# Lightning attention and a feed-forward network: the states of the first groups in PSUM banks of their own, decayed from PSUM, with a new order of operations

## The chip, the cores and the metric

The kernel runs on one core of one Trainium2 chip. The metric is device time in microseconds (us), lower is better. A core has five engines with an instruction queue each: TensorE (PE in the profile, and PEld for its weight loads), VectorE (DVE), ScalarE (ACT), GpSimd (POOL) and SyncE (SP, which here issues most transfers). They share the on-chip memory SBUF. TensorE writes its products to PSUM, which holds eight banks here; VectorE and ScalarE can read PSUM.

A time of a run is some 1.7 to 2 us longer than its span, which goes from the first to the last instruction. Each run records the mean granted clock of TensorE, 1.0 being full speed.

## The reference

Attention without softmax, in blocks, with a decayed state; then a feed-forward network with the activation h + sin²(alpha·h)/alpha. Cut to what matters:

```python
# q, k, v: 4 batches x 8 heads x 768 positions x 64;  lam: one decay per head
for b in range(nb):                                   # blocks of 64 positions
    intra = einsum(einsum(qb, kb) * Dmask, vb)        # inside the block
    inter = einsum(qb * lam_pow, kv_state)            # what earlier blocks left
    out[:, :, block] = intra + inter
    kv_state = lam**64 * kv_state + einsum(kb * rev_pow, vb)

x = out, as 3072 rows x 512
h = x @ w_in                                          # 512 -> 2048
g = h + sin(alpha * h)**2 / alpha
return g @ w_out                                      # 2048 -> 512
```

## The kernel before

The kernel works in 24 attention units of 4 heads by 256 positions (two chunks of 128, numbered 0 and 1). Four units make a group of 512 rows, and each of the six groups goes through the feed-forward network. Nothing is scheduled automatically: one list, ORDER, gives every operation, its engine and its place, and each engine takes its own operations in that order. A wait of one operation therefore holds up everything behind it on that engine.

An entry is `operation.indices:engine:bank`, with engines V (VectorE), G (GpSimd), A (ScalarE), T (TensorE), S (SyncE). The names that the text uses are these:

| entry | what it does |
|---|---|
| `ld`, `wi`, `wo` | loads of q, k, v of a unit; of a quarter of w_in; of a quarter of w_out |
| `sq`, `sk`, `cv` | scale q and k by powers of lam, cast v to bf16 |
| `tq`, `tk`, `tcq`, `tck` | turn q and k on TensorE, and copy the result out of PSUM (`tdq`, `tdk`: turn by DMA) |
| `s`, `m` | scores (16 matmuls), and their mask on VectorE |
| `k`, `kc` | matmuls of the chunks' states, and their copy from PSUM to SBUF |
| `a.u.c`, `n.u.c` | add the earlier state and decay it for the output; make the state that the next chunk takes |
| `o`, `x` | output of the unit, and its copy to the rows that the network reads |
| `f1`, `sin`, `sqr`, `stt`, `f2` | first product, sine, square, the rest of the activation, second product (`f1a`: half of an `f1`, with the first two units of a group alone) |
| `w.n` | n filler matmuls on zeros, whose result nobody reads |

Before, the states of both chunks are written into a spare part of `okv`, a pair of PSUM banks (one for each chunk) that the outputs use too. They are copied to SBUF together, and everything after that has SBUF inputs:

```python
def kvmm(u, **_):
    okv[u] = ps.tile([P, 2, 512], FP32, name="okv", tag="okv", bufs=1)
    ...                                                # 16 matmuls into okv[u]

def kv_copy(u, eng, **_):
    kva[u] = kvp.tile([P, 2, 2, D], FP32, name=f"kva{b}{hh}", bufs=1)
    copy(eng, kva[u][:, :n]..., okv[u][:, :n, 2 * P:3 * P])      # both chunks

def kv_decayed(u, c, eng, **_):
    x = kva[u][:, c]                                   # in SBUF
    if prev is not None:
        eng.tensor_tensor(out=t[:], in0=x, in1=prev[:], op=ALU.add)
        x = t[:]
    eng.tensor_tensor(out=kvbd[u, c][:], in0=x..., in1=LBD..., op=ALU.mult)

def load(u, j, **_):
    loads[u, j] = nc.sync.dma_start(...)
    if 4 <= u < 8 and j == 0 and mlp[0] is not None:   # mlp: the last feed-forward
        after(loads[u, j], mlp[0])                     # matmul written so far
```

In ORDER the units of group 1 (4 to 7) are mixed into group 0 and into the first product, and several state operations and scalings stand on VectorE while GpSimd works too. The loads of units 4 to 7 come early and don't wait, since no feed-forward matmul stands before them. The quarters of w_in are spread out:

```
... m.1.1:V wi.0:G w.3:T:okv o.0:T ... k.3:T a.1.0:V sk.4:V sq.4:G ... wi.1:G tck.3:V
s.3:T k.4:T tcq.4:V kc.4:A ... n.1.0:V a.4.0:G ... o.3:T s.4:T x.3.0:V x.3.1:A
f1a.0.0:T:1 f1.0.0:T f1a.0.1:T:3 sq.6:G m.4.0:V m.4.1:V wi.2:G sk.6:G tq.5:T:0 ...
```

Of the kernel before, what the change touches and what calls it, by code (L numbers as in the profile page):

```python
# [11 lines left out]
FP32 = mybir.dt.float32  # L12
# [6 lines left out]
ld.0.0:S ld.0.1:S ld.0.2:S ld.1.0:S ld.1.1:S ld.1.2:S ld.2.0:S ld.2.1:S ld.2.2:S ld.3.0:S sq.0:G  # L19
ld.3.1:S ld.3.2:S ld.4.0:S ld.4.1:S tq.0:T:2 sk.0:V tk.0:T:0 sq.1:V cv.0:A sk.1:G tables:V k.0:T  # L20
cv.1:G sq.2:G tq.1:T:3 kc.0:V tcq.1:V sk.2:G w.5:T:h1 tk.1:T:1 tck.1:A k.1:T tcq.0:V tck.0:V s.0:T
m.0.0:V a.0.0:G m.0.1:V kc.1:V tq.2:T:0 w.4:T:h2 tk.2:T:2 cv.2:A k.2:T kc.2:A tck.2:A s.1:T ld.4.2:S
ld.5.0:S ld.5.1:S sq.3:V ld.5.2:S ld.6.0:S ld.6.1:S cv.3:G ld.6.2:S ld.7.0:S ld.7.1:S ld.7.2:S
ld.8.0:S sk.3:G tcq.2:A m.1.0:V m.1.1:V wi.0:G w.3:T:okv o.0:T x.0.0:V tq.3:T:3 tcq.3:A w.3:T:s0
s.2:T w.4:T:okv k.3:T a.1.0:V sk.4:V sq.4:G tk.3:T:3 m.2.0:V m.2.1:V kc.3:A w.3:T:okv o.1:T cv.4:A
x.1.0:A tq.4:T:0 a.3.0:G a.2.0:G sk.5:G wi.1:G tck.3:V s.3:T k.4:T tcq.4:V kc.4:A n.0.0:G tk.4:T:2
m.3.0:V tck.4:A sq.5:G m.3.1:V w.3:T:okv o.2:T a.0.1:G n.1.0:V a.4.0:G cv.5:G x.2.0:A w.5:T:okv
o.3:T s.4:T x.3.0:V x.3.1:A f1a.0.0:T:1 f1.0.0:T f1a.0.1:T:3 sq.6:G m.4.0:V m.4.1:V wi.2:G sk.6:G
tq.5:T:0 f1a.0.2:T:2 tk.5:T:5 f1.0.1:T cv.6:G tcq.5:V f1.0.2:T sin.0.0:A n.2.0:G sqr.0.0:A a.1.1:V
sq.7:G stt.0.0:V sin.0.1:A sqr.0.1:V sin.0.2:A sqr.0.2:A n.1.1:G n.4.0:G k.5:T stt.0.1:V tck.5:V  # L30
kc.5:V stt.0.2:V f1a.0.3:T:4 f1.0.3:T f1.0.4:T:0 sin.0.3:A sin.0.4:A sqr.0.3:A sqr.0.4:V wi.3:G
f1.0.5:T:1 stt.0.3:V sin.0.5:A sk.7:G wo.0:G f1.0.6:T:3 stt.0.4:V a.5.0:G sqr.0.5:A f1.0.7:T:2 s.5:T
k.6:T stt.0.5:V sin.0.6:A sqr.0.6:A kc.6:V m.5.0:V tq.6:T:0 tcq.6:A sin.0.7:A sqr.0.7:A w.4:T:okv
o.4:T stt.0.6:V m.5.1:V stt.0.7:V x.4.0:A cv.7:A tk.6:T:4 f1.0.8:T:1 f1.0.9:T:0 k.7:T tq.7:T:3
kc.7:V ld.8.1:S ld.8.2:S tcq.7:V tk.7:T:2 ld.9.0:S tck.6:A sin.0.8:A sqr.0.8:V s.6:T sin.0.9:A
m.6.0:V tck.7:A o.5:T m.6.1:V wo.1:G n.3.0:G a.7.0:G sqr.0.9:A ld.9.1:S ld.9.2:S ld.10.0:S ld.10.1:S
x.5.0:A stt.0.8:V f1.0.10:T:3 stt.0.9:V f1.0.11:T:2 a.6.0:G s.7:T sin.0.10:A o.6:T sin.0.11:A
m.7.0:V sqr.0.10:A f1.0.12:T:1 f1.0.13:T:0 sqr.0.11:G sq.8:G sin.0.12:A x.6.0:A sin.0.13:A
f1.0.14:T:4 sin.0.14:A stt.0.10:V m.7.1:V sqr.0.12:V sqr.0.13:G stt.0.11:V stt.0.12:V stt.0.13:V
o.7:T sqr.0.14:G f1.0.15:T:3 stt.0.14:V x.7.0:A f1a.1.0:T:5 f1.1.0:T sin.0.15:A sqr.0.15:A sin.1.0:A  # L40
f1a.1.1:T:2 f1.1.1:T f1a.1.2:T:1 f1a.1.3:T:4 f1.1.2:T sqr.1.0:A sin.1.1:A sin.1.2:A sqr.1.1:A
n.7.0:V stt.0.15:V a.3.1:V sqr.1.2:A n.5.0:G sk.8:G n.0.1:G f2.0.1.0:T:0 stt.1.0:V f1.1.3:T wo.2:G
f1.1.4:T:3 sin.1.3:A f1.1.5:T:5 stt.1.1:V sqr.1.3:A sin.1.4:A sqr.1.4:A stt.1.2:V stt.1.3:V
f2.0.2.0:T:2 a.4.1:G sq.9:G cv.8:G stt.1.4:V k.8:T wo.3:G n.6.0:G sk.9:G tdq.8:S sin.1.5:A
f2.0.1.1:T tdq.9:S tdk.8:S cv.9:A sqr.1.5:A stt.1.5:V f1.1.6:T:4 sin.1.6:A f1.1.7:T:3 sin.1.7:A
f2.0.0.0:T:1 f2.0.0.1:T f1.1.8:T:5 sqr.1.6:A sq.10:G sk.10:G stt.1.6:V kc.8:V a.8.0:G sin.1.8:A
sqr.1.7:A ld.10.2:S cv.10:G a.2.1:V sqr.1.8:A stt.1.7:V a.5.1:V a.7.1:V stt.1.8:V f2.0.1.2:T k.9:T
kc.9:A f2.0.0.2:T f2.0.0.3:T ld.11.0:S n.8.0:G n.4.1:G tdk.9:S ld.11.1:S ld.11.2:S oc.0.0:A
ld.12.0:S ld.12.1:S f1.1.9:T:3 f2.0.1.3:T sin.1.9:A k.10:T s.8:T n.3.1:V sqr.1.9:A tdq.10:S
f1.1.10:T:1 f2.0.2.1:T stt.1.9:V m.8.0:V n.2.1:V tdk.10:S ld.12.2:S sk.11:G sq.11:G tdq.11:S  # L50
tdk.11:S f2.0.2.2:T ld.13.0:S m.8.1:V cv.11:A kc.10:A sin.1.10:A ld.13.1:S ld.13.2:S ld.14.0:S
oc.0.1:V f1.1.11:T:3 k.11:T sin.1.11:A sqr.1.10:A sqr.1.11:A sk.12:G kc.11:A s.9:T m.9.0:V m.9.1:V
f2.0.2.3:T stt.1.10:V f2.0.3.0:T:0 cv.12:A oc.0.2:A st.0.2.0:S ld.14.1:S s.10:T ld.14.2:S st.0.1.0:S
a.10.0:G sq.12:G a.9.0:G o.8:T m.10.0:V x.8.0:V m.10.1:V f2.0.3.1:T f1.1.12:T:1 stt.1.11:V o.9:T
sin.1.12:A x.9.0:V n.5.1:G s.11:T a.11.0:G ld.15.0:S ld.15.1:S ld.15.2:S f1.1.13:T:2 o.10:T sk.13:G
sin.1.13:A x.10.0:A m.11.0:V m.11.1:V cv.13:A sqr.1.12:A f1.1.14:T:3 a.8.1:G f1.1.15:T:5 sin.1.14:A
sqr.1.13:A sin.1.15:A sq.13:G a.6.1:V ld.16.0:S ld.16.1:S tdq.12:S ld.16.2:S o.11:T f2.0.3.2:T
sq.14:G sk.14:G x.11.0:V f2.0.3.3:T stt.1.12:V stt.1.13:V oc.0.3:V sqr.1.14:A k.12:T kc.12:A
f1.2.0:T:4 f1.2.1:T:2 stt.1.14:V f1.2.2:T:1 sqr.1.15:G stt.1.15:V f1.2.3:T:3 f1.2.4:T:0 n.9.0:G
sin.2.0:A sin.2.1:A sqr.2.0:A stt.2.0:V sin.2.2:A sqr.2.1:A stt.2.1:V cv.14:G sk.15:G sin.2.3:A  # L60
k.13:T ld.17.0:S tdk.12:S kc.13:V sk.16:G sin.2.4:A sqr.2.2:A stt.2.2:V sqr.2.3:G n.11.0:G ld.17.1:S
stt.2.3:V f1.2.5:T:4 sqr.2.4:A stt.2.4:V n.6.1:V n.10.0:G f1.2.6:T:5 sin.2.5:A f1.2.7:T:2 f1.2.8:T:1
f1.2.9:T:3 sq.15:G a.12.0:G n.12.0:G f2.1.0.0:T:0 f2.1.0.1:T sq.16:G sin.2.6:A sin.2.7:A sqr.2.5:A
sin.2.8:A sqr.2.6:A sqr.2.7:A stt.2.5:V stt.2.6:V sin.2.9:A sqr.2.8:A sqr.2.9:G n.7.1:G st.0.0.0:S
a.13.0:G cv.15:G tdq.13:S stt.2.7:V k.14:T s.12:T ld.17.2:S tdk.13:S m.12.0:V m.12.1:V f2.1.0.2:T
tdq.14:S tdq.15:S st.0.0.1:S kc.14:A f2.1.0.3:T o.12:T sq.17:G ld.18.0:S a.10.1:G stt.2.8:V
stt.2.9:V s.13:T a.12.1:G f2.1.1.0:T:2 a.14.0:G n.8.1:G x.12.0:V st.0.2.1:S tdk.14:S m.13.0:V
f1.2.10:T:1 f1.2.11:T:3 tdq.16:S st.0.1.1:S m.13.1:V oc.1.0:V tdk.15:S tdk.16:S st.0.3.0:S o.13:T
ld.18.1:S ld.18.2:S ld.19.0:S ld.19.1:S ld.19.2:S ld.20.0:S ld.20.1:S s.14:T x.13.0:A cv.16:A
m.14.0:V f2.1.1.1:T sin.2.10:A m.14.1:V f2.1.1.2:T k.15:T kc.15:V sqr.2.10:G stt.2.10:V sq.18:G  # L70
f1.2.12:T:0 sin.2.11:A sqr.2.11:A stt.2.11:V n.12.1:G tdq.17:S f2.1.1.3:T cv.17:A oc.1.1:A o.14:T
s.15:T m.15.0:V n.14.0:G f1.2.13:T:3 sin.2.12:A sqr.2.12:A a.15.0:G a.9.1:G tdq.18:S x.14.0:V
f1.2.14:T:2 ld.20.2:S ld.21.0:S ld.21.1:S ld.21.2:S k.16:T f1.2.15:T:1 stt.2.12:V m.15.1:V
f2.1.2.0:T:0 kc.16:A o.15:T f2.1.2.1:T f2.1.2.2:T f2.1.2.3:T sin.2.13:A sqr.2.13:A sin.2.14:A
a.16.0:G x.15.0:A sqr.2.14:G stt.2.13:V n.10.1:G sk.17:G stt.2.14:V f1.3.0:T:2 k.17:T n.13.0:G
cv.18:G sq.19:G n.15.0:G s.16:T st.1.1.0:S sin.2.15:A sqr.2.15:A stt.2.15:V oc.1.2:V f1.3.1:T:0
sin.3.0:A sin.3.1:A sqr.3.0:A sqr.3.1:A a.15.1:G f2.1.3.0:T:3 f2.1.3.1:T tdk.17:S st.0.3.1:S sk.18:G
tdq.19:S f2.1.3.2:T n.9.1:G m.16.0:V a.14.1:G f2.1.3.3:T m.16.1:V f1.3.2:T:1 kc.17:A k.18:T
stt.3.0:V stt.3.1:V s.17:T m.17.0:V m.17.1:V sin.3.2:A a.11.1:G sk.19:G sqr.3.2:G cv.19:G f1.3.3:T:0
f1.3.4:T:2 f1.3.5:T:4 oc.1.3:A sin.3.3:A sqr.3.3:A kc.18:V n.11.1:G n.15.1:G stt.3.2:V stt.3.3:V  # L80
f1.3.6:T:3 f1.3.7:T:1 f1.3.8:T:5 sin.3.4:A sqr.3.4:A sin.3.5:A sqr.3.5:G stt.3.4:V sin.3.6:A
sqr.3.6:G stt.3.5:V stt.3.6:V sin.3.7:A st.1.2.0:S st.1.0.0:S o.16:T ld.22.0:S ld.22.1:S f1.3.9:T:0
f1.3.10:T:4 f2.2.0.0:T:2 f2.2.0.1:T f1.3.11:T:3 f2.2.0.2:T sqr.3.7:A ld.22.2:S st.1.0.1:S ld.23.0:S
ld.23.1:S ld.23.2:S cv.20:A stt.3.7:V x.16.0:V sin.3.8:A sqr.3.8:A sin.3.9:A stt.3.8:V sqr.3.9:A
stt.3.9:V a.18.0:G f2.2.0.3:T k.19:T sin.3.10:A a.13.1:G a.17.0:G sin.3.11:A sqr.3.10:G tdk.19:S
stt.3.10:V sqr.3.11:A st.1.3.0:S tdk.18:S kc.19:V s.18:T m.18.0:V stt.3.11:V sq.20:G f2.2.1.0:T:0
o.17:T sk.20:G sk.21:G x.17.0:A m.18.1:V f1.3.12:T:1 f1.3.13:T:3 f2.2.1.1:T st.1.3.1:S s.19:T
m.19.0:V sq.21:G o.18:T f2.2.1.2:T sq.22:G sk.22:G f1.3.14:T:4 x.18.0:V k.20:T kc.20:V cv.21:A
sin.3.12:A oc.2.0:A f1.3.15:T:2 k.21:T sqr.3.12:G sin.3.13:A sin.3.14:A n.13.1:G sqr.3.13:G
f2.2.1.3:T a.19.0:G m.19.1:V kc.21:A sqr.3.14:A stt.3.12:V a.20.0:G stt.3.13:V tdq.20:S n.14.1:G  # L90
# [33 lines left out]
def kernel(  # L124
# [11 lines left out]
    nc = tc.nc  # L136
# [464 lines left out]
```

## Time and profile before

| | before |
|---|---|
| timed runs | 231.43 us, median of 3 (230.57 to 232.22) |
| profiled run | 228.56 us, span 226.8 us, clock 0.992 |
| TensorE busy | 211.3 us, 93% of the span |
| first feed-forward matmul | 25.59 us |

From the profile page of the kernel before: busy time of each engine; below it the span in 40 slices of 5.67 us, a digit being the busy share in tenths, and for PEclk the granted clock in tenths.

```profile
PE 211.3 (93%) x2081; PEld 110.3 (49%) x2111; DVE 139.2 (61%) x231; ACT 126.3 (56%) x219; POOL 135.5 (60%) x195
...
PE   8587877999999999989999999999999999999993
...
DVE  3979699788578977867546755256583563524020
...
PEclk9969999999999999999999999999999999999999
```

TensorE is the limit, and it is full nearly everywhere but in the first seven slices (to 40 us). In the third slice the clock was cut: the 6 is a stretch of half clock.

The timeline of VectorE in the kernel before, from 16 to 32 us: start, duration in us, engine, line, operation, output<-inputs, their shapes and the number of instructions; in brackets the idle time before it and what ended it.

```profile
17.08 1.86 DVE L398 TENSOR_TENSOR kvbd<-kva,LBD 128x256 bf16<-128x256 f32 x1
...
22.79 1.20 DVE L406 TENSOR_TENSOR kvs<-kva,LHP 128x128 f32<-128x128 f32 x1
...
27.85 3.12 DVE L394 TENSOR_TENSOR kvx<-kva,kvs 128x128 f32<-128x128 f32 x1
31.01 0.42 DVE L398 TENSOR_TENSOR kvbd<-kvx,LBD 128x256 bf16<-128x256 f32 x1
```

The timeline of GpSimd in the same kernel from 26 to 32 us, with the same columns:

```profile
27.87 1.05 POOL L277 TENSOR_TENSOR KD<-st_k,R 128x512 bf16<-128x512 f32 x1
28.86 0.62 POOL L270 CAST VB<-st_v 128x512 bf16<-128x512 f32 x1
29.43 0.40 POOL L406 TENSOR_TENSOR kvs<-kva,LHP 128x128 f32<-128x128 f32 x1
29.79 1.03 POOL L277 TENSOR_TENSOR QL<-st_q,E 128x512 bf16<-128x512 f32 x1
```

The same decay took 1.86 us once and 0.42 us the other time. The addition at 27.85 us took 3.12 us, about as long as four GpSimd instructions that followed each other without a gap (27.87 to 30.82 us). The Trainium skill, page "SBUF — State Buffer", section "Who interferes with whom", says that a VectorE instruction with two inputs in SBUF contends with a GpSimd instruction that reads SBUF, and that one with at most one SBUF input, outside the two-port modes, doesn't. The trace agrees.

The timeline of TensorE in the kernel before, from 24 to 34 us:

```profile
25.59 1.59 PE L453 MATMUL hps<-xt,w_in_sb 128*128 128x256 bf16 x12
...
30.64 1.04 PE L453 MATMUL hps<-xt,w_in_sb 128*128 128x512 bf16 x3 [0.47 <-DMA w_in_sb<-in_moe_w_in_dram]
32.15 1.02 PE L453 MATMUL hps<-xt,w_in_sb 128*128 128x512 bf16 x4 [0.47 <-DVE gall L487]
```

The first product begins at 25.59 us, mixed with group 1, and waits for a piece of w_in and then for VectorE, whose late `stt` (gall) hold the PSUM banks.

### The profile page before, as it was taken

Reading aid. Unit: us, or ns where it says so; the run is one execution under the profiler, and the core shown is the slowest. Engines: PE = TensorE matmul, PEld = TensorE weight load, DVE = VectorE, ACT = ScalarE, POOL = GpSimd, SP = SyncE. Lnnn points to the kernel's source line nnn. Section 1 sums busy time; section 2 is a strip of 40 time slices with the busy share of each in tenths; the row PEclk is TensorE's granted clock in tenths of the full one; section 3 lists DMA queues with packets and bytes.
Section 4 is the critical chain, followed back from the end, with each engine's and each line's share of the span. In section 5 each row is a group of like instructions: output and inputs, shape, how many; then the busy total and the mean of one; then the engine's idle time right before and its main releaser. Section 6 shows DMA issues by size and latency. Waiting matters only on the chain.

```text
span 226.8 us, 5334 instructions
## 1 busy us (share of the span) xinstructions
PE 211.3 (93%) x2081; PEld 110.3 (49%) x2111; DVE 139.2 (61%) x231; ACT 126.3 (56%) x219; POOL 135.5 (60%) x195
## 2 busy tenths in 40 slices
PE   8587877999999999989999999999999999999993
PEld 6365644565444544544444444444555444444452
DVE  3979699788578977867546755256583563524020
ACT  2234468989667479644648853468345376553101
POOL 5669994389656799897897999246152153530000
PEclk9969999999999999999999999999999999999999
DMA  5999999956999999798999915504015022132235
GB/s 140 291 293 242 268 268 251 216 110 99 141 258 182 289 287 202 180 134 219 220 248 260 194 27 111 112 13 90 21 28 116 3 46 46 25 72 46 44 71 117
DMA packets 63849, 33.92 MB, mean 150 GB/s; under 512 B 19648, under 2 KB 60880, under 8 KB 63824
## 3 DMA queue, kind: packets, MB, share of 16 engines
q1 hardware_dynamic: 59344, 29.31, 58.5%
q0 software_dynamic: 4224, 4.19, 11.5%
q8 instruction: 16, 0.26, 0.5%
q10 hardware_dynamic: 256, 0.08, 0.2%
q14 instruction: 9, 0.07, 0.1%
HBM read 27.28 MB, written 6.29 MB: 148 GB/s over the span
## 4 chain that ended last, share of the span: by engine, by line
PE 77%; DVE 9%; DMA 4%; POOL 3%; issue 2%; ACT 2%; SPq 1%; DVEq 0%; ACTq 0%; POOLq 0%
PE ops L496 33%; PE hps L453 31%; PE okv L430 3%; PE sp L345 3%; DMA QT<-KD 2%; PE okv L421 2%; PE okv L376 2%; DVE gall L487 2%; DMA lam_bc<-in_lam_dram 2%; PE ops L519 2%; DVE kvx L394 1%; PE bz L563 1%; DVE ST L355 1%; DVE kvbd L398 1%; POOL QL L277 1%
## 5 line engine op out<-in xcount | busy, mean ns | idle before, releaser
L487 DVE SCALAR_TENSOR_TENSOR gall<-s,r_sb,hps 128x512 bf16<-128x512 bf16 x96 | 69.4, 743 | 41.7 <-POOL s L482 23.0
L453 PE MATMUL hps<-xt,w_in_sb 128*128 128x512 bf16 (+1 forms) x399 | 89.9, 362 | 2.2 <-DVE gall L487 0.9
L473 ACT ACTIVATE s<-hps,alpha_sb 128x512 bf16<-128x512 f32 x96 | 64.8, 686 | 40.7 <-PE hps L453 35.7
L496 PE MATMUL ops<-w_out_sb,gall 128*128 128x512 bf16 x355 | 84.4, 379 | 1.3 <-issue 0.9
L482 POOL TENSOR_TENSOR s<-s 128x512 bf16<-128x512 bf16 x32 | 33.1, 1041 | 45.0 <-ACT s L473 44.8
L453 PEld LDWEIGHTS <-w_in_sb 128*128 128x128 bf16 x416 | 38.7, 98 | 41.4 <-issue 1.2
L496 PEld LDWEIGHTS <-gall 128*128 128x128 bf16 x368 | 34.7, 98 | 40.6
L355 DVE TENSOR_TENSOR ST<-sp,mask 128x512 bf16<-128x512 f32 x48 | 31.5, 683 | 13.6 <-PE sp L345 13.5
L480 ACT ACTIVATE s<-s 128x512 bf16<-128x512 bf16 x60 | 36.6, 626 | 1.2 <-DVE gall L487 0.4
L277 POOL TENSOR_TENSOR KD<-st_k,R 128x512 bf16<-128x512 f32 x22 | 22.9, 1045 | 5.5 <-DMA st_k<-in_k_dram 4.2
L277 POOL TENSOR_TENSOR QL<-st_q,E 128x512 bf16<-128x512 f32 x22 | 22.9, 1044 | 0.4 <-DVE E L217 0.3
L268 ACT COPY ob<-ops 128x512 f32<-128x512 f32 (+1 forms) x14 | 7.8, 554 | 23.4 <-PE ops L496 14.0
L398 POOL TENSOR_TENSOR kvbd<-kvx,LBD 128x256 bf16<-128x256 f32 x26 | 16.1, 619 | 2.0
L268 ACT CAST xt<-okv 128x512 bf16<-128x512 f32 (+1 forms) x15 | 8.5, 568 | 13.6 <-PE okv L430 11.6
L270 DVE COPY ob<-ops 128x512 f32<-128x512 f32 x11 | 7.5, 685 | 13.2 <-PE ops L496 13.1
L394 POOL TENSOR_TENSOR kvx<-kva,kvs 128x128 f32<-128x128 f32 x26 | 12.2, 468 | 3.8 <-DVE kva L270 2.0
L345 PE MATMUL sp<-QT 64*64 64x128 bf16 x384 | 10.4, 226 | 2.3 <-DVE QT L270 1.3
L268 ACT CAST VB<-st_v 128x512 bf16<-128x512 f32 x13 | 8.0, 615 | 6.7 <-DMA st_v<-in_v_dram 6.7
L430 PE MATMUL okv<-ST,VB 64*64 64x128 bf16 x384 | 10.0, 222 | 0.0
L345 PEld LDWEIGHTS <-QT 64*64 64x64 bf16 x384 | 6.9, 111 | 5.3 <-issue 2.5
L376 PEld LDWEIGHTS <-KD 64*64 64x64 bf16 x320 | 5.2, 109 | 8.1 <-issue 3.6
L270 POOL CAST VB<-st_v 128x512 bf16<-128x512 f32 x11 | 6.7, 612 | 3.7 <-DMA st_v<-in_v_dram 3.7
(60 smaller groups left out, 138.0 us busy)
## 6 DMA issues: line engine op xcount, KB each, us to landing
st_q<-in_q_dram SPq DMA_DIRECT2D x24, 256.0 KB, 5.5
st_k<-in_k_dram SPq DMA_DIRECT2D x24, 256.0 KB, 5.4
st_v<-in_v_dram SPq DMA_DIRECT2D x24, 256.0 KB, 5.2
out_dram<-ob SPq DMA_DIRECT2D x46, 128.0 KB, 2.4
w_in_sb<-in_moe_w_in_dram POOLq DMA_DIRECT2D x4, 512.0 KB, 8.8
w_out_sb<-in_moe_w_out_dram POOLq DMA_DIRECT2D x4, 512.0 KB, 9.3
QT<-QL SPq DMA_TRANSPOSE x16, 3.9
QT<-KD SPq DMA_TRANSPOSE x16, 3.9
```

What stands on the lines that cost most here:

```text
L268: nc.scalar.copy(out=out, in_=in_)
L277: eng.tensor_tensor(out=t[:], in0=stage[u, j][:].rearrange("p h two e -> p two h e"), in1=tab[:, :, hh * HH:(hh + 1) * HH].unsqueeze(3).to ...
L345: nc.tensor.matmul(out=sp[hd][half[c], par, hp, :], lhsT=QT[half[hd], 1, par, hp, half[c]], rhs=QT[half[hd], 0, :, hp, half[c]], start=Tru ...
L355: nc.vector.tensor_tensor(out=stm[u][:, hd], in0=sps[u][hd][:], in1=mask[:].unsqueeze(2).to_broadcast([P, 2, 2, P]), op=ALU.mult)
L398: eng.tensor_tensor(out=kvbd[u, c][:], in0=x.unsqueeze(2).to_broadcast([P, 2, 2, D]), in1=LBD[:, 2 * hh:2 * hh + 2, :].unsqueeze(3).to_bro ...
L430: nc.tensor.matmul(out=okv[u][half[hd], c, hp * P:(hp + 1) * P], lhsT=VB[half[c], par, 2 * hp + hd, :], rhs=ST[half[c], hd, par, hp, :], s ...
L453: mlp[0] = nc.tensor.matmul(out=hps[g, f][:].rearrange("p (b i) -> p b i", b=2)[:, bs] .rearrange("p b i -> p (b i)"), lhsT=w_in_sb[:, c, ...
L473: nc.scalar.activation(out=s1[g, f][:], in_=hps[g, f][:], func=ACTF.Sin, scale=alpha_sb[:, f:f + 1])
L480: nc.scalar.activation(out=s2[g, f][:], in_=x[:], func=ACTF.Square)
L482: eng.tensor_tensor(out=s2[g, f][:], in0=x[:], in1=x[:], op=ALU.mult)
L487: nc.vector.scalar_tensor_tensor(out=gall[g][:, f, :], in0=s2.pop((g, f))[:], scalar=r_sb[:, f:f + 1], in1=hps.pop((g, f))[:], op0=ALU.mul ...
L496: mlp[0] = nc.tensor.matmul(out=ops[g, m][:], lhsT=gall[g][:, f, m * P:(m + 1) * P], rhs=w_out_sb[:, f, :], start=(f == 0), stop=(f == NFC ...
```

## The change

The intent: take work from the port that VectorE and GpSimd share, and get group 0 finished sooner. The diff, cut to its core:

```diff
-    XSPLIT = (3,)
+    HOLD = (0, 1)
+    XSPLIT = (2, 3)
 ...
-    nc.scalar.dma_start(out=lam_bc[:], in_=lam.partition_broadcast(P))
+    nc.sync.dma_start(out=lam_bc[:], in_=lam.partition_broadcast(P))
 ...
+    (tables LHP, LBD, and later alpha_sb, r_sb: now made at the start,
+     before, by an operation "tables" in ORDER)
 ...
-        if 4 <= u < 8 and j == 0 and mlp[0] is not None:
-            after(loads[u, j], mlp[0])
+        if (u, j) == (4, 0):
+            after(loads[u, j], f1mm[HOLD])
 ...
-    def kvmm(u, **_):
-        okv[u] = ps.tile([P, 2, 512], FP32, name="okv", tag="okv", bufs=1)
+    def kvmm(u, bank, **_):
+        if u < 8:
+            kps[u] = [psum([P, P], FP32, "kvp", i)[:] for i in bank]
+        else:
+            okv[u] = ps.tile([P, 2, 512], FP32, name="okv", tag="okv", bufs=1)
+            kps[u] = [okv[u][:, c, 2 * P:3 * P] for c in range(2)]
 ...
     def kv_decayed(u, c, eng, **_):
-        x = kva[u][:, c]
+        if u < 8 and c == 0:
+            x = kps[u][0].rearrange("p (hp e) -> p hp e", hp=2)
+        else:
+            x = kva[u][:, c]
```

The copy `kc.u.c` of units 0 to 7 now takes one chunk, and the output copies of unit 2 are split by chunk, as those of unit 3 were. ORDER is new throughout. Units 0 to 3 are all but finished before the first product; units 4 to 7 stand inside the second product of group 0; loads of unit 4 and later wait until the fourth matmul of `f1.0.1`, so the quarters of w_in, now issued one after the other, have the DMA engines with less company. The head of the new order, cut:

```
... k.0:T:3,0 tck.0:V sk.1:V s.0:T a.0.0:V m.0.0:V ... k.1:T:2,1 s.1:T o.0:T sk.2:G kc.0.0:A sq.2:V ...
... m.2.1:V wi.0:G wi.1:G a.0.1:G wi.2:G wi.3:G k.2:T:0,1 ... f1a.0.0:T:4 o.3:T f1a.0.1:T:3 ...
f1.0.6:T:3 f1.0.7:T:0 f1.0.8:T:1 f1.0.9:T:4 f1.0.10:T:2 ... ld.4.0:S ld.4.1:S ld.4.2:S ...
... f2.0.2.0:T:2 tq.4:T:5 f2.0.0.0:T:3 ... k.4:T:3,0 ... o.4:T ... o.7:T ... f1a.1.0:T:4 ...
```

## The prediction

> **What bounds the kernel now.** TensorE. The page gives PE 211.3 us busy of a 226.8 us span (93%). The groups and the chain of waits give throughputs: four 512-column matmuls take 0.86 us, so both feed-forward products need 768 x 0.2155 = 165.5 us. An attention unit costs about 0.35 (scores) + 0.65 (output) + 0.25 (states), times 24; transposes 3.5 us: useful PE work is about 199 us. The tail after the last matmul is 3.9 us. About 23.5 us is lost, 7.4 before the first transpose.
>
> Counting matmuls by stretch of time, 29.3 us of useful work is done by 50.2 us: 13.5 us is lost between 7.4 and 50.2, some 3 us in the remaining 170. The first feed-forward matmul starts at 25.6 us.
>
> **Why the head is slow.** In the timeline VectorE is nearly dense from 6.5 to 37 us, with instructions stretched: one 128x128 state addition took 3.12 us (GpSimd's are 0.47), a state decay 1.86 (GpSimd 0.62), a key scaling 1.35 (another 0.68), a 64x4 copy 1.03 (its twin 0.16). Each overlaps GpSimd instructions. This agrees with the Trainium skill, page "SBUF — State Buffer", section "Who interferes with whom": VectorE instructions with two SBUF inputs, or in a two-port mode, and GpSimd block each other. The excess sums to about 7 us by 31 us.
>
> **What the change does.** In groups 0 and 1 VectorE decays the first state straight from PSUM (estimate 0.42 us) without waiting for the copy; state additions go to GpSimd; two banks per unit free the output's bank. The tables move before the first scaling, where VectorE waits for GpSimd's first scaling (to about 7.3 us): the first key scaling comes 1 us later. Group 0 now precedes the first product, which runs almost unmixed; group 1 is mixed into the second. Loads of units 4 to 7 wait for an early feed-forward matmul, so w_in lands sooner.
>
> VectorE's list up to group 0's last masks sums to 14 us. From 7.3 us, by hand, group 0 ends and full feed-forward starts near 22 to 23 us, with 7.3 us of useful work done: 7.5 to 8.5 us lost, against about 11 lost at 25.6 us before. Gain: 2.5 to 3.5 us. The unmixed first product (16 x 0.86 = 13.8 us) balances ScalarE at about 13.7, so about 1 us is lost. Group 1 amid the second product is VectorE-dense and lies at the edge of DMA: loads of eight units and both weights need about 51 us of all DMA engines (shares of the queue table), so unit 7 lands about 48. I expect 2 to 3 us lost there, as before from 25.6 to 50. The rest stays within 1.5 us.
>
> **Predicted: 228.5 us (225.0 to 231.8).** Faster by over 2%: 0.28; within 2%: 0.69; slower: 0.03.
>
> **What would show it.** Right: no VectorE state instruction above 0.8 us before 40 us; VectorE's busy time falls by about 7 us; full feed-forward starts at 21.5 to 23.5 us; PE stays above 97% after 60 us. Wrong: feed-forward starting at 25 us or later, PE waiting for w_in between 22 and 33 us, or for unit 6 or 7 loads between 42 and 52 us.
>
> **What would make it wrong.** The VectorE chain may be latency-bound, delaying the head; group 1 may fit perfectly under the second product (then 225 or below); the granted clock (0.66 at 10 to 15 us) may change; new stalls later.

## The result, and the profile after

| | before | after |
|---|---|---|
| timed runs, median | 231.74 us (230.57 to 232.22, 4 runs) | 223.67 us (222.35 to 224.02, 4 runs) |
| ratio, with 95% interval | | 0.9649 (0.9594 to 0.9703) |
| profiled run | 228.56 us, span 226.8, clock 0.992 | 223.69 us, span 221.9, clock 1.000 |

Ratios here and below are the mean time of one kernel's fast runs over that of the other's of the same rounds, so they are not quite the ratio of the medians quoted. The change is faster by 3.5%, some 8 us, and lies below the predicted range. The profiled runs alone show only 4.9 us of it.

From the profile page of the kernel after, the lines that answer to those above (a slice is 5.55 us):

```profile
PE 208.5 (94%) x2081; PEld 109.3 (49%) x2111; DVE 128.0 (58%) x220; ACT 129.6 (58%) x234; POOL 132.2 (60%) x200
...
PE   8689999799999999999979999999999999999992
...
DVE  3996698158699758674658475757531362580020
...
PEclk9999999999999999999999999999999999999999
```

TensorE is full from the fourth slice on, but for two slices at seven tenths: the 8th (39 to 44 us) and the 21st (111 to 117 us), which before were nearly full at these places. The clock is never cut, and VectorE is busy 11.2 us less.

The state tiles of the kernel after, `kvp` in PSUM: all decays that read them, with minimum, median and maximum in ns and the first and last start.

```profile
L420 DVE TENSOR_TENSOR kvbd<-kvp,LBD x8: 408/416/425, 10.0 to 53.6; 128x256 bf16<-128x256 f32 x8
```

All eight took 0.41 to 0.43 us, six of them (at 10.01 and 19.86 us and the four of group 1, from 47.73 us on) beside GpSimd instructions: the case with one SBUF input doesn't contend, as the page says. The run a_decay_sbuf below shows the same decays from SBUF. One blocked instruction is left on VectorE; its timeline from 9 to 13 us:

```profile
10.01 0.42 DVE L420 TENSOR_TENSOR kvbd<-kvp,LBD 128x256 bf16<-128x256 f32 x1
10.34 1.28 DVE L364 TENSOR_TENSOR ST<-sp,mask 128x512 bf16<-128x512 f32 x2
11.54 1.45 DVE L286 TENSOR_TENSOR QL<-st_q,E 128x512 bf16<-128x512 f32 x1
```

The scaling of q at 11.54 us has two SBUF inputs and runs beside a scaling on GpSimd (11.39 to 12.43 us); its twin at 8.47 us took 0.68.

TensorE of the kernel after, timeline from 18 to 46 us:

```profile
20.16 0.60 PE L475 MATMUL hps<-xt,w_in_sb 128*128 128x256 bf16 x4
...
21.15 13.79 PE L475 MATMUL hps<-xt,w_in_sb 128*128 128x256 bf16 x75
34.78 1.03 PE L518 MATMUL ops<-w_out_sb,gall 128*128 128x512 bf16 x3
...
41.31 3.61 PE L518 MATMUL ops<-w_out_sb,gall 128*128 128x512 bf16 x15 [1.25 <-DMA w_out_sb<-in_moe_w_out_dram]
```

From 21.15 us the first product runs in one piece without a wait, and the second begins where it ends. One wait of 1.25 us for the last w_out follows.

### Where TensorE loses time, stage by stage

To compare two orders, I credited each matmul in the trace with its time at full throughput (0.2155 us per 512 columns, 0.35 us per 16 score or output matmuls, 0.25 us per 16 state matmuls, fillers nothing). This sums to 195.6 us for either kernel. "Lost" is the clock on the wall less the useful work done, cut at fixed amounts of useful work. The first 8 us of useful work are about group 0 and its transposes; from 8 to 20 is the first product, mixed with group 1 in the order before; from 20 to 44 the second product. The tail after the last matmul, about 4 us in both, is left out.

```
lost us     to first    to 8     to 20    to 44    to 62    to       sum
            transpose   useful   useful   useful   useful   end
before        7.41      11.07     4.09     0.57     0.47     3.44    27.0   (profiled run)
c_before      7.46      14.34     3.76     0.57     0.47     4.24    30.8   (before, run again)
after         6.90       7.66     0.13     2.03     0.78     4.69    22.2
c_after       6.97       7.65     0.13     2.70     0.78     5.19    23.4   (after, run again)
```

Against the profiled run of before, the head gained 3.9 us with its start, the first product 4.0, and 3.0 were given back later. Against a more usual run of before (the next section), the head gained 7.2.

### The profile page after: what moved, and what is told of

It is laid out like the page before. It is cut to its first block, busy times and chain, and to the rows that moved or that the text cites. A ratio compares the mean times of both kernels' runs of the same rounds, so it can differ in the third digit from the quotient of the medians.

```text
span 221.9 us, 5359 instructions
## 1 busy us (share of the span) xinstructions
PE 208.5 (94%) x2081; PEld 109.3 (49%) x2111; DVE 128.0 (58%) x220; ACT 129.6 (58%) x234; POOL 132.2 (60%) x200
## 4 chain that ended last, share of the span: by engine, by line
PE 74%; DMA 12%; POOL 4%; issue 3%; SPq 2%; DVE 1%; ACT 1%; POOLq 0%; ACTq 0%
PE ops L518 31%; PE hps L475 29%; DMA w_out_sb<-in_moe_w_out_dram 6%; PE okv L452 3%; PE sp L354 3%; DMA QT<-QL 2%; PE okv L443 2%; PE bz L576 2%; PE ops L541 2%; PE pt L313 2%; DMA st_k<-in_k_dram 2%; SPq L533 1%; PE okv L390 1%; DMA lam_bc<-in_lam_dram 1%; POOL E L212 1%
## 5 line engine op out<-in xcount | busy, mean ns | idle before, releaser
L509 DVE SCALAR_TENSOR_TENSOR gall<-s,r_sb,hps 128x512 bf16<-128x512 bf16 x96 | 68.2, 744 | 37.7 <-ACT s L502 23.7
L475 PE MATMUL hps<-xt,w_in_sb 128*128 128x512 bf16 (+1 forms) x402 | 87.9, 362 | 1.2 <-issue 0.6
L504 POOL TENSOR_TENSOR s<-s 128x512 bf16<-128x512 bf16 x26 | 26.9, 1038 | 35.6 <-ACT s L495 35.5
L502 ACT ACTIVATE s<-s 128x512 bf16<-128x512 bf16 x63 | 39.0, 629 | 1.0
L416 POOL TENSOR_TENSOR kvx<-kva,kvs 128x128 f32<-128x128 f32 x32 | 14.5, 454 | 11.6 <-ACT kva L277 9.2
L420 POOL TENSOR_TENSOR kvbd<-kvx,LBD 128x256 bf16<-128x256 f32 x32 | 19.6, 612 | 2.5
L277 ACT CAST xt<-okv 128x512 bf16<-128x512 f32 (+1 forms) x18 | 10.0, 553 | 9.9 <-PE okv L452 9.8
L279 POOL CAST VB<-st_v 128x512 bf16<-128x512 f32 x14 | 8.9, 642 | 3.3 <-DMA st_v<-in_v_dram 3.3
L428 POOL TENSOR_TENSOR kvs<-kvx,LHP 128x128 f32<-128x128 f32 x24 | 9.6, 407 | 0.0
L279 DVE CAST xt<-okv 128x512 bf16<-128x512 f32 (+1 forms) x8 | 5.3, 657 | 6.6 <-PE okv L452 5.2
```

The source lines that it names most:

```text
L277: nc.scalar.copy(out=out, in_=in_)
L279: eng.tensor_copy(out=out, in_=in_)
L420: eng.tensor_tensor(out=kvbd[u, c][:], in0=x.unsqueeze(2).to_broadcast([P, 2, 2, D]), in1=LBD[:, 2 * hh:2 * hh + 2, :].unsqueeze(3).to_bro ...
L475: f1mm[g, f] = nc.tensor.matmul(out=hps[g, f][:].rearrange("p (b i) -> p b i", b=2)[:, bs] .rearrange("p b i -> p (b i)"), lhsT=w_in_sb[:, ...
L502: nc.scalar.activation(out=s2[g, f][:], in_=x[:], func=ACTF.Square)
L504: eng.tensor_tensor(out=s2[g, f][:], in0=x[:], in1=x[:], op=ALU.mult)
```

## The experiments

The theories were these. A: what counts is the contention of VectorE with GpSimd, which moving some operations away from VectorE would cure alone. B: what counts is the order, with group 0 done first and w_in loaded before the next units. C: the two banks count. D: part of the gain is TensorE's clock, since gaps in the head of before throttle it (the expectations of the two clock runs call this one theory C). Fifteen kernels were run; all gave correct results. Kernels named b_ start from before (but b_order, which is an edit of after), those named a_ from after. They ran in four sets of rounds on two chips, each set with its own runs of before, to which its ratios refer.

### The kernel before, again

No edit.

> The kernel before, unchanged, as a control. The traces of before and after differ by only 4.9 us of span (226.8 against 221.9), the timed medians by 8.1 us (231.74 against 223.67), because the profiled run of before (228.56 us) was faster than all of its timed runs (230.57 to 232.22). If that profiled run was a lucky one, this control's timed runs are again 230 to 232 us and its second profile shows a span near 229 to 230 us with the extra 3 us in one place, probably a longer stretch of halved clock in the first 25 us. If before simply has a wide spread, some timed runs fall near 228.5 us.

Measured: 231.67 us (230.40 to 232.79), ratio 1.004 (0.9976 to 1.0104); the profiled run has a span of 230.6 us at a clock of 0.976. The windows view of c_before, in windows of 3.4 us: window, its length, busy time and instructions of each engine, granted clock, DMA share and GB/s.

```profile
15.00:18.40 3.40, 3.04 (x67) 1.97 (x65) 1.90 (x5) 1.55 (x4) 3.30 (x4) 1.00 1.15 285
18.40:21.80 3.40, 1.44 (x25) 0.86 (x24) 3.40 (x4) 1.11 (x2) 2.27 (x4) 0.98 1.04 202
21.80:25.20 3.40, 3.07 (x57) 2.18 (x58) 2.08 (x5) 1.04 (x3) 3.30 (x6) 0.50 1.17 302
25.20:28.60 3.40, 2.79 (x41) 1.83 (x41) 0.57 (x2) 0.61 (x2) 3.38 (x6) 0.50 1.21 227
28.60:32.00 3.40, 3.40 (x20) 2.56 (x19) 1.53 (x4) 1.57 (x3) 2.51 (x4) 0.52 1.19 303
```

From 21.6 to 31.9 us the clock is halved, 10.2 us long. In the window before it TensorE was busy for 1.44 of 3.4 us. What stopped it, from VectorE's timeline of c_before:

```profile
18.34 2.01 DVE L277 TENSOR_TENSOR KD<-st_k,R 128x512 bf16<-128x512 f32 x1 [1.37 <-DMA st_k<-in_k_dram]
20.27 1.27 DVE L355 TENSOR_TENSOR ST<-sp,mask 128x512 bf16<-128x512 f32 x2
21.47 0.74 DVE L270 COPY QT<-pt 128x512 bf16<-128x512 bf16 x2
```

And TensorE's:

```profile
21.93 0.64 PE L345 MATMUL sp<-QT 64*64 64x128 bf16 x16 [2.00 <-DVE QT L270]
```

The scaling of unit 4's keys (`sk.4:V`) stands at the head of VectorE's queue. It waits 1.37 us for its load, then takes 2.01 us beside GpSimd. The masks and copies of group 0 stand behind it, and TensorE waits 2.00 us for them. The Trainium skill, page "TensorE: Matmul & The Clock Gate", section "Part 1: The HAM clock gate", describes a clock that is either full or half, decided over windows of 3.413 us, and restored after at least one busy window. The trace agrees with the half (0.50) and with the size: the halved stretches that I measured lasted 3.4, 6.8, 10.2 and 13.7 us. Here three windows passed, with TensorE busy for 3.07, 2.79 and 3.40 us of them, and the full clock came back after the one that was full; so this doesn't contradict the page.

In the profiled run of before the same thing happened once, and for one window. The windows view of the kernel before, around it:

```profile
8.20:11.60 3.40, 2.07 (x48) 1.27 (x45) 3.32 (x12) 0.59 (x1) 2.65 (x4) 1.00 1.18 294
11.60:15.00 3.40, 3.21 (x60) 2.35 (x60) 2.30 (x5) 0.79 (x2) 1.57 (x2) 0.51 1.24 295
```

The clock was no accident of one run. In all 36 runs of before beside the experiments it lay between 0.974 and 0.990 (mean 0.980; median time 230.89 us); in ten runs of after it lay between 0.996 and 1.000 (mean time 223.41 us). A straight line through the 36 runs gives 1.6 us per 0.01 of clock, and 227.7 us at full clock; through the 29 fast ones alone, 1.3 us and 228.0 us. The correlation is only -0.55 (-0.50), so this is an estimate: some 3 of the 8 us are clock. The profiled run of before (0.992) had a higher clock than any of them, and only one of them was faster (227.84 us, at 0.985).

### Contention alone

b_states_pool is the kernel before with three state operations moved to GpSimd; b_letters4 moves the key scaling of unit 4 as well:

```diff
-a.1.0:V ... n.1.0:V ... a.1.1:V
+a.1.0:G ... n.1.0:G ... a.1.1:G
-sk.4:V          (b_letters4 only)
+sk.4:G
```

> The kernel before with only three state operations (the first decay and next state of unit 1 and the second addition and decay of unit 1) moved from VectorE to GpSimd, which took 1.86, 1.20, 3.12 and 0.42 us on VectorE beside GpSimd. Theory A (VectorE instructions with two SBUF inputs blocked beside GpSimd make the head's loss): VectorE gets about 5 us back before 32 us, the stalls of the first feed-forward product between 29 and 35 us shrink, and the time falls by 2 to 4 us. Rival B (the order of the groups is what counts; the first product mixed with group 1 has to stall anyway): within 1 us of before.

> As the run with three state operations moved to GpSimd, and the key scaling of unit 4 moved to GpSimd too. In the control and in that run this scaling stood in VectorE's queue ahead of the work of units 2 and 3, waited 1.4 to 2.2 us for its load and then took 2.0 to 2.4 us beside GpSimd (0.6 to 0.7 elsewhere). If this is what idles TensorE for 2 us before the scores of unit 3: that wait falls below 0.8 us, the clock is at least 0.99 and the median is 225.5 to 227.5 us, 3 to 5 below before. If the order of the groups is what counts: 228 to 229 us, as with the three.

Measured: b_states_pool 228.52 us (227.90 to 231.10), ratio 0.9926 (0.9854 to 0.9999), clock 0.985 in the profiled run; b_letters4 228.38 us (228.04 to 228.68), ratio 0.9889 (0.9845 to 0.9934), clock 0.985. Lost up to 8 us of useful work and from there to 20: 13.85 and 2.04 us, then 12.80 and 1.69 us, against 14.34 and 3.76 in c_before.

The moves are worth little: by the ratios 1.7 and 2.6 us (of 231) out of 8. The first product gains 2 us, as `stt` comes in time. The head keeps nearly all its loss: 6.8 us of half clock stay in both. That contention is what these moves cure is not shown. In c_before the same decay, next state and addition took 0.48, 0.47 and 0.28 us, so they weren't stretched like that, and yet that run was 3.8 us slower than the profiled run of before, where they took 1.86, 1.20 and 3.12 us. And moving `sk.4` also removes its wait for a load from VectorE's queue.

### Order, banks, and decaying from PSUM

b_order is the kernel after, but with the states of both chunks in the pair `okv` again, one copy for both right behind the matmuls, and decays from SBUF. a_decay_sbuf keeps the two banks, and only lets the decay read the copy, so copies move up behind their matmuls:

```diff
 b_order:
-        if u < 8:
-            kps[u] = [psum([P, P], FP32, "kvp", i)[:] for i in bank]
-        else:
-            okv[u] = ...
+        okv[u] = ps.tile([P, 2, 512], FP32, name="okv", tag="okv", bufs=1)
+        kps[u] = [okv[u][:, c, 2 * P:3 * P] for c in range(2)]
 b_order and a_decay_sbuf:
-        if u < 8 and c == 0:
-            x = kps[u][0].rearrange("p (hp e) -> p hp e", hp=2)
-        else:
-            x = kva[u][:, c]
+        x = kva[u][:, c]
```

> The kernel after with its order, tables, held loads and early lam, but with the states of all units in the single pair of banks as before, both chunks copied at once right behind the matmuls, and VectorE decaying the first state from that SBUF copy. Theory A with the PSUM decays as an essential part: 2 to 4 us slower than after, with some VectorE decays stretched above 0.8 us before 22 us. Rival B (order): within 1 us of after, since VectorE has slack in the new order of the head.

> The kernel after, two banks kept, but VectorE decays the first state of units 0 to 7 from the SBUF copy, which is now made before it, instead of from PSUM. If reading from PSUM matters (shorter chain and no wait beside GpSimd), 1 to 2.5 us slower than after and decays above 0.8 us where GpSimd runs; if not, within 0.7 us. Together with the run that also gives up the two banks it splits the two halves of that part of the change.

Measured: b_order 228.32 us (226.62 to 229.50, and one slow run of 233.03), ratio 0.9896 (0.9806 to 0.9987), full clock in the profiled run; a_decay_sbuf 224.72 us (223.30 to 225.36), ratio 0.9732 (0.9676 to 0.9788). The median of b_order includes its slow run; its three fast runs have a mean of 227.75 us, the four of a_decay_sbuf 224.53. The two intervals just miss each other, and every fast run of b_order is slower than every run of a_decay_sbuf: in the new order the separate banks are worth 3.2 us between these means (one of the three had a clock of only 0.985), and 2.0 us between the spans of the profiled runs, both at nearly full clock (224.8 and 222.8). TensorE of b_order shows what the shared pair costs:

```profile
18.27 0.32 PE L386 MATMUL okv<-VB,KD 64*64 64x64 bf16 x16 [1.65 <-ACT xt L276]
...
21.25 0.32 PE L386 MATMUL okv<-VB,KD 64*64 64x64 bf16 x16 [0.75 <-ACT xt L276]
```

The state matmuls of units 2 and 3 wait until the last output has been copied out of the banks that they share. Theory C holds in the new order, where units follow each other closely; in the order of before it was not tried. Decaying from PSUM rather than from the copy is worth about 1 us (224.72 against 223.67 and 223.31 for the kernel after), and as the intervals of a_decay_sbuf and of c_after (0.9651 to 0.9757) overlap, this rests on the trace. VectorE's timeline of a_decay_sbuf:

```profile
19.41 0.43 DVE L417 TENSOR_TENSOR kvbd<-kva,LBD 128x256 bf16<-128x256 f32 x1 [1.31 <-ACT kva L277]
```

And TensorE's:

```profile
19.89 0.29 PE L440 MATMUL okv<-QT,kvbd 128*128 128x128 bf16 x2 [0.85 <-DVE kvbd L417]
```

This decay from SBUF took 0.43 us, no longer than from PSUM, but GpSimd ran no instruction beside it. So here the gain of reading PSUM is not the port: it is one copy less in the chain. The port shows where GpSimd is at work. The timeline of VectorE in a_decay_sbuf, with the first decay of the head and of group 1, and GpSimd's at the second place:

```profile
10.27 0.58 DVE L417 TENSOR_TENSOR kvbd<-kva,LBD 128x256 bf16<-128x256 f32 x1 [0.16 <-ACT kva L277]
...
48.30 1.12 DVE L417 TENSOR_TENSOR kvbd<-kva,LBD 128x256 bf16<-128x256 f32 x1
...
48.10 1.04 POOL L286 TENSOR_TENSOR QL<-st_q,E 128x512 bf16<-128x512 f32 x1 [0.23 <-PE kvp L390]
```

And the same decay of group 1 in the kernel after, from PSUM:

```profile
47.73 0.42 DVE L420 TENSOR_TENSOR kvbd<-kvp,LBD 128x256 bf16<-128x256 f32 x1
```

The four decays of group 1 took 1.12, 0.52, 0.87 and 0.89 us from SBUF, and 0.41 to 0.42 from PSUM. This is the expected "above 0.8 us where GpSimd runs", but it cost TensorE little: counted as in the table above, a_decay_sbuf loses 1.2 us more than the kernel after in the head, where the copy counts, and 0.3 us more from 20 to 44 us of useful work.

### Clock

b_fill adds 23 filler matmuls to the kernel before, at its three holes. a_nofill takes all 34 from the kernel after:

```diff
 b_fill:
-s.0:T
+w.5:T:s0 s.0:T
-s.3:T
+w.14:T:h1 s.3:T
-o.3:T
+w.4:T:h1 o.3:T
 a_nofill:
-w.2:T:h1 ... w.5:T:h2 ... w.7:T:h2 ... w.6:T:h1 ... w.2:T:okv ... w.7:T:s0 ... w.5:T:s0
```

> The kernel before with 23 more filler matmuls on zeros (some 2.8 us of TensorE work, put where TensorE sat idle in the control: 5 before the first scores, 14 before the scores of unit 3, 4 before the output of unit 3); nothing else changed. Theory C (new, from the control's trace: VectorE's stalls leave TensorE idle for 2 us, 42% busy over 3.4 us, and the granted clock falls to half for 3.4 to 10 us, which is what differs between the profiled runs and costs before about 3 us): the clock stays at 1.00 or 0.99, the median falls by 1.5 to 3.5 us in spite of the extra work. If the halved clock is harmless or is not set by idle TensorE: the same or slower by up to 1 us.

> The kernel after without its 34 filler matmuls between real ones (the 28 at the start stay). Theory C: the mean granted clock falls below 0.99, with a stretch of half clock between 10 and 25 us, and the time rises by 1.5 to 4 us. Rival (the fillers only fill idle time, the new order keeps TensorE busy enough by itself): within 0.7 us of after, clock 0.996 or 1.00.

Measured: b_fill 229.47 us (227.48 to 229.69, and one slow run of 233.36), ratio 0.9903 (0.9840 to 0.9967), clock 1.000 in the profiled run; a_nofill 226.85 us (225.13 to 227.89), ratio 0.9811 (0.9753 to 0.9870), clock 0.962 to 0.970 in all four runs. The windows view of a_nofill:

```profile
7.00:10.40 3.40, 1.88 (x44) 1.31 (x43) 3.21 (x10) 0.84 (x2) 0.97 (x1) 0.82 1.22 292
10.40:13.80 3.40, 2.92 (x65) 1.91 (x58) 3.39 (x7) 1.24 (x5) 2.52 (x4) 0.50 1.14 274
```

The half clock begins at 9.2 us and lasts 13.7 us. Theory D holds: useless matmuls are worth about 2.2 us in the order before (0.97% of 231) and 3.2 us in the order after. The change itself adds no filler; it places the same 34 where they cover its gaps. With them, the same two windows of the kernel after read:

```profile
7.00:10.40 3.40, 2.58 (x56) 1.79 (x56) 3.33 (x11) 0.64 (x2) 0.90 (x1) 1.00 1.21 294
10.40:13.80 3.40, 2.88 (x67) 1.97 (x65) 3.40 (x6) 2.09 (x6) 2.44 (x4) 1.00 1.12 268
```

### The held loads

a_nohold lets unit 4 and later load as soon as they can:

```diff
-        if (u, j) == (4, 0):
-            after(loads[u, j], f1mm[HOLD])
```

> The kernel after with the loads of units 4 to 7 no longer held until an early feed-forward matmul; they start behind those of unit 3, at about 10 us. If holding them is essential to get w_in in time: TensorE waits for w_in between 22 and 33 us, 1 to 4 us slower. If not: within 0.7 us, or up to 1.5 us faster, because the waits for w_out and for the loads of unit 6 between 38 and 50 us (2 us lost) shrink or grow with the order in which the transfers come.

Measured: 227.02 us (226.36 to 227.72), ratio 0.9827 (0.9783 to 0.9870), 3.4 to 3.7 us slower than the kernel after. The profiled run was at full clock (span 225.5 against 221.9 us), the other three at 0.989 to 0.991, so a part of their time may be clock. TensorE of a_nohold:

```profile
22.32 0.61 PE L473 MATMUL hps<-xt,w_in_sb 128*128 128x256 bf16 x4 [2.24 <-DMA w_in_sb<-in_moe_w_in_dram]
```

Its four pieces of w_in land at 22.28, 25.88, 29.57 and 33.17 us; in the kernel after at 19.10, 21.64, 25.04 and 27.71 us, and in the profiled run of before at 24.23, 30.59, 36.5 and 40.6 us. The Trainium skill, page "DMA: Bandwidth & Descriptors", section "SWDGE vs HWDGE vs iDMA", says that transfers issued by GpSimd and those issued by SyncE feed different internal queues, between which a DMA engine takes turns. The landings fit this, though they would fit any sharing of the DMA engines: w_in (GpSimd) comes 3.2 to 5.5 us later when the loads (SyncE) are not held. This part of the change is a line or two of code, and its removal costs as much as that of any other part.

### The load of lam

a_lam_act lets ScalarE issue the load of lam again, as before:

```diff
-    nc.sync.dma_start(out=lam_bc[:], in_=lam.partition_broadcast(P))
+    nc.scalar.dma_start(out=lam_bc[:], in_=lam.partition_broadcast(P))
```

> The kernel after with the small load of lam issued from ScalarE's queue again, as in before. In after the power that starts the whole head began at 3.85 us, in before at 4.36 us. If the issuing queue is the reason: it begins at 4.3 to 4.4 us here, the first transpose moves from 6.9 to 7.4 us, and the time rises by about 0.5 us (0.2 to 1.0). If the loads' landing sets the start instead: no change above 0.2 us.

Measured: 223.19 us (222.35 to 224.40), ratio 0.9722 (0.9667 to 0.9776), so the same as the kernel after (c_after, in another set of rounds: 0.9704). The first transpose comes at 7.43 us rather than 6.90, and the second product starts 0.82 us later, but part of this is taken back by a shorter wait for w_out (the loss from 20 to 44 us of useful work is 1.60 against 2.03 us) and the rest later (3.60 against 4.69). A gain of half a microsecond at the start did not arrive at the end.

### All small edits on the kernel before

b_all has the four letters of b_letters4, 21 fillers (`w.5` before `s.0`, `w.12` before `tq.4`, `w.4` before `o.3`) and the load of lam on SyncE.

> The kernel before with everything that can be had by small edits: the four VectorE operations on GpSimd, 21 fillers against the halved clock, and lam on the first queue. The order of the groups, the unheld loads and the single banks stay as before. If contention and clock explain the gain of the change: 223.5 to 225 us, near after. If the order with w_in loaded first is what gives most of it (my theory now): 226 to 228 us, because the first product still cannot start before w_in lands at about 24 us and its second to fourth parts come at 30 to 40 us.

Measured: 228.87 us (226.52 to 232.32, two of six runs slow), ratio 0.9933 (0.9844 to 1.0022), although all its clocks lie between 0.993 and 1.000. Its profiled run has a span of 225.1 us and still loses 11.60 us up to the first product. The small edits don't add up: the interval holds the gain of any one of them. The four fast runs lie between 226.52 and 228.92 us, and the two slow ones (231.71 and 232.32) had clocks of 1.000 and 0.993, so what slowed these two is not the mean clock; it was not found.

### Attempts at a better kernel

a_best1 moves two DMA turns of unit 17 up (TensorE of the kernel after waits for them at 114 us) and one part of the second product earlier. a_best2 adds to it the copy of alpha on ScalarE, the reciprocal later, and q and k of unit 2 exchanged between VectorE and GpSimd, to remove the one blocked instruction. a_hyb and a_hyb2 take the head of after (a_hyb2 that of a_best2) up to the end of `f1.1`, and the order of before from there. c_after is the kernel after, unedited.

```diff
 a_best1:
-f2.0.1.2:T f2.0.2.2:T f2.0.0.1:T
+f2.0.0.1:T f2.0.1.2:T f2.0.2.2:T
-st.1.1.0:S ... ld.18.0:S tdq.17:S ... ld.19.1:S tdk.17:S
+tdq.17:S tdk.17:S st.1.1.0:S ... ld.18.0:S ... ld.19.1:S
 a_best2, on top:
-sk.2:G ... sq.2:V
+sq.2:G ... sk.2:V
-    nc.vector.tensor_copy(out=alpha_sb[:], in_=ap[:])
+    nc.scalar.copy(out=alpha_sb[:], in_=ap[:])
```

> The kernel after with two moves in its order: the two turning transfers of unit 17 ahead of the four stores that stand before them in the queue (TensorE waited 1.49 us for one of them before the scores of unit 17), and one piece of the second product that needs only the landed part of w_out put ahead of the piece that waited 1.25 us for a later part. Expected 1.5 to 2.3 us faster than after (221.4 to 222.2 us); if TensorE only waits elsewhere for the same transfers, 0 to 0.5 us.

> As the run before, with the copy of alpha made by ScalarE (0.43 us less in VectorE's chain before the first key scaling) and the two scalings of unit 2 exchanged between VectorE and GpSimd (in after VectorE's took 1.45 us beside GpSimd's, twice its usual 0.68). Expected: the first feed-forward matmul starts 0.4 to 1.2 us earlier than in after and the time falls by the same amount against the run before. If w_in's landing (19.1 us in after) takes over, only 0 to 0.4 us.

> The kernel after, unchanged, as a control beside its variants. If the first measurement holds: 222.3 to 224.0 us, clock 0.996 or 1.00. If the chip of this call differs: about 224.4 us, and the last two variants were then no slower than after.

> The kernel after up to the end of its third attention group and second first-product, then before's order for all the rest. If before's later order is the better one by what the traces show (3.4 us lost there from that point against 4.7): 0.8 to 1.6 us faster than the control of after. If the later losses follow from the head's state (loads and states that come later in after), the same within 0.7 us.

> The same with the variant of after's head that has alpha copied by ScalarE and the scalings of unit 2 exchanged. Its profile showed the head 0.2 us ahead of after at the start of the second product. Expected: within 0.5 us of the hybrid before it; 1.0 to 2.0 us faster than the control of after if both gains add.

| kernel | median us (range) | ratio (95%) |
|---|---|---|
| c_after | 223.31 (222.53 to 224.96) | 0.9704 (0.9651 to 0.9757) |
| a_best1 | 224.39 (223.83 to 226.24) | 0.9782 (0.9725 to 0.9838) |
| a_best2 | 224.41 (223.45 to 226.70) | 0.9785 (0.9718 to 0.9852) |
| a_hyb | 233.99 (233.43 to 235.29) | 1.0175 (1.0122 to 1.0228) |
| a_hyb2 | 234.15 (233.59 to 234.79) | 1.0178 (1.0124 to 1.0232) |

None beats the kernel after. TensorE of the kernel after at 114 us, with the wait that a_best1 meant to remove:

```profile
114.04 0.42 PE L354 MATMUL sp<-QT 64*64 64x128 bf16 x16 [1.49 <-DMA QT<-KD]
```

TensorE of a_best1 at the same place:

```profile
114.87 0.34 PE L443 MATMUL okv<-QT,kvbd 128*128 128x128 bf16 x3 [0.40 <-POOL kvbd L420]
```

The wait of 1.49 us is gone, and the next ones appear: for a decay on GpSimd at 114.87 us, and for others in the units after. a_best2 did shorten the blocked scaling from 1.45 to 0.68 us, and the head gained only 0.3 us (7.35 us lost rather than 7.66), which was lost again later. The hybrids fail at the seam. TensorE of a_hyb:

```profile
80.78 3.20 PE L475 MATMUL hps<-xt,w_in_sb 128*128 128x512 bf16 x8 [2.49 <-DVE gall L509]
89.35 3.57 PE L475 MATMUL hps<-xt,w_in_sb 128*128 128x512 bf16 x8 [5.37 <-DVE gall L509]
```

This is the wait for `stt` before a bank comes free. The head of after postpones state operations that the order of before expects to be done; piled up, they kept GpSimd busy without a gap from 75 to 91 us with state operations and scalings, and its squares, for which VectorE's `stt` waits, came late. 11.9 us are lost there, with the clock halved for 10.2 us of it. Past the seam the order of before loses 3.54 us to the end, as it did at home (3.44), and less than that of after (4.69).

## Why the prediction was wrong

It said 228.5 us with a range of 225.0 to 231.8; the result is 223.67 us. The mechanism was largely right, and the sum was wrong. It promised a gain of 3.2 us where 8.1 were measured; 1.6 of the missing 4.8 us lie in the stages of the two profiled runs, and 3.2 in what a usual run of before takes beyond its profiled one. By stages of the two profiled runs, the gain in us is 3.9 (start and head) + 2.5 (both products of group 0: 4.66 lost before, 2.16 after) - 1.6 (the rest: 3.91 before, 5.47 after), which is the 4.9 us between the spans, up to rounding. The other 3.2 us or so are the head of a usual run of before (11.07 us lost in the profiled run, 14.34 in c_before).

- **The step that failed: "I expect 2 to 3 us lost there, as before from 25.6 to 50."** For the kernel after the 2 to 3 us were right (2.03 us). "As before" was not: before loses about 4.7 us there, of which 4.09 in the first product mixed with group 1. The term came from a count of useful work, "29.3 us of useful work is done by 50.2 us"; counted again from the trace the value is 27.2 (probably the half-size first products were taken too high). So 2 us of loss were hidden, and the prediction credited the unmixed first product with nothing. It measured 0.13 us lost ("about 1 us is lost", it said).
- **The clock was named and not counted.** "The granted clock (0.66 at 10 to 15 us) may change" stood under what would make the prediction wrong, with no value. The profile of before was a lucky run, faster than all the timed runs beside it, which the numbers at hand already said. The mean clock of 0.980 in the 36 runs of before means about 9 us at half clock (0.020 of some 229 us, times two), and c_before shows 10.2 us. b_fill and a_nofill measure what the clock is worth: about 2 us in the order before and 3 us in the order after.
- **Holding the loads was named and not counted.** "So w_in lands sooner" is true (the last piece at 27.71 rather than 40.6 us), and undoing it alone costs 3.4 us.
- **The two banks were given no value of their own.** In the new order they are worth 2.0 us of span and 3.2 us between the means of the fast runs.
- **The contention was read right, and its share was smaller than the text suggests.** No state instruction of VectorE took over 0.8 us before 40 us, as it said. Its busy time fell by 11.2 us, not 7. But moving the blocked instructions away alone is worth 1.7 to 2.6 us. In the head of the new order, decays from SBUF took 0.41 to 0.58 us; in group 1 they did stretch, to 1.12 us, at little cost.
- **The head was right for the profiled run.** It foresaw 7.5 to 8.5 us lost and full feed-forward at 21.5 to 23.5 us; measured are 7.66 us and 21.15 us, a little earlier than it said.
- **Other signs.** Unit 7 was to land at about 48 us; its loads landed at 47.3 to 49.07 us, and TensorE did not wait for them, only for w_out (1.25 us). "PE stays above 97% after 60 us" is wrong: from 110 to 120 us TensorE was busy for 8.35 of 10 us in the kernel after (9.80 in that of before), as unit 17's turn came late.

The values of the undone parts (3.4 for the loads, 3.2 for the fillers, 2.0 to 3.2 for the banks, 1 for the PSUM decay) don't sum to the gain, since each undone part opens gaps that the others had closed, and the fillers were there before. What the new order is worth without the held loads, the separate banks and the fillers in its gaps was not run, so the order by itself (theory B) has no measured value.

Two things stay open. Two of the six runs of b_all were some 4 us slower than the rest, at clocks of 1.000 and 0.993, for a cause that these runs don't show. And the new order loses about 1.6 us more than the profiled old one after the second product; neither moving single waits nor joining the two orders got it back.

## What to carry to other kernels

Compare the profiled run with the timed ones before building a sum on it: a profile that is faster than every timed run hides a loss; here the granted clock of the other runs named it, once they were listed. A change of order should be costed stage by stage in lost TensorE time, with small matmuls counted at their own size, since "as before" is a number too. When each engine works through a fixed list, an operation that waits for a load must not stand ahead of the work that TensorE needs next; hold back loads that aren't needed yet, give short-lived results a bank of their own, and fill the holes that are left, so that the clock stays up.

## What the Trainium skill lacked or had wrong

- Page "TensorE: Matmul & The Clock Gate": its table lets the clock fall after an idle window, and another of its sections after frequent short idles; it gives no share of busy time for either, nor for the busy window that restores the clock. Here a window in which TensorE was busy for 1.44 of 3.4 us was followed by half clock, and so was one with 2.07 of 3.4 us in the profiled run of before. These runs don't settle a share. In the traces cut along the changes of the clock into windows of 3.413 us, half clock followed full-clock windows with 0.51 to 2.04 us busy, but windows with 1.97 (b_letters4) and 2.02 us (a_nohold) kept the full clock. It came back after half-clock windows with 2.70 (a_hyb) and 2.80 us (a_hyb2), but not after one with 3.10 us (a_nofill).
- Page "SBUF — State Buffer": it says that the first to start has the shared ports for its whole instruction while the other is blocked. It doesn't say that several instructions can pass a waiting one: here one VectorE addition of 128x128 elements took 3.12 us while four GpSimd instructions (1.05, 0.62, 0.40 and 1.03 us) ran one behind the other.
- Page "DMA: Bandwidth & Descriptors": it gives no figure for what a transfer of GpSimd loses beside those of SyncE. Here holding back the SyncE loads brought the w_in pieces 3.2 to 5.5 us sooner.
